# Loading the first keys by two other queues at the start of a sigmoid-attention and mixer kernel

## The chip, the cores and the metric

The kernel runs on one core of a Trainium2 chip. The metric is the device time of one execution in microseconds (us), given as the median of several runs. A core has five engines with a queue of instructions each: PE (matrix products and transposes, with its weight loads shown as PEld), DVE (vector), ACT (scalar, activation functions), POOL (general), and SP (here only issues DMAs). Sixteen DMA engines move data. SBUF is the memory on the chip that tiles live in; PSUM holds PE's results.

## The reference

Eight batches, 12 heads, 448 positions, 64 elements a head. Sigmoid attention comes first, and its result, with the heads side by side (768 columns), goes through a mixer block without normalization.

```python
def _attn_ref(q, k, v):
    S = q.shape[2]
    scale = 1.0 / np.sqrt(q.shape[-1])
    scores = scale * np.matmul(q, k.transpose(0, 1, 3, 2)) - np.log(S)
    attn = 1.0 / (1.0 + np.exp(-scores))
    return np.matmul(attn, v).astype(np.float32)

def _moe_ref(x, w_tok1, w_tok2, w_ch1, w_ch2):
    xt = x.transpose(0, 2, 1)
    h = np.maximum(xt @ w_tok1, 0.0) @ w_tok2
    u = x + h.transpose(0, 2, 1)
    h2 = np.maximum(u @ w_ch1, 0.0) @ w_ch2
    return u + h2
```

All inputs and the output are fp32. w_tok1 is 448 x 256, w_tok2 256 x 448, w_ch1 768 x 1536, w_ch2 1536 x 768.

## The kernel before, in words

The batches are worked on in five units: "A" and "B" are one batch each, and 1, 2 and 3 are two batches each. A unit is handled in pairs of heads: three pairs for A and B, six for the others. In a pair a tile holds the keys (or queries, or values) of two heads on each of two sides of the 128 partitions. A position is written as p*7+j, so that partition p holds seven rows, j = 0 to 6, and one step of the attention is one j: four matmuls of scores (L423), one sigmoid on ACT (L430) over 128 x 896 elements, and four matmuls of values (L441) that add up over j.

Keys and queries must be turned first, so that the 64 elements of a head lie across partitions. For the first seven pairs (`BY_PE = 7`) PE turns them (`turn_by_pe`, L345): 14 transposes against the identity matrix `ident`, into one PSUM bank, and one copy by DVE to SBUF. For later pairs POOL reorders the tile (`permute`, L337, tiles pk and pq) and SP issues a DMA transpose (`turn_by_dma`, L362).

Loads are issued by POOL (`load`, L238), two DMAs a tile, one for each side. The source is fp32 and the tile fp16; the DMA casts. The very first keys are loaded by `load_first` (L255) in two parts, j = 0 to 2 and j = 3 to 6 (`KEYS`), so that scores can begin on the first part. Each part is turned by `turn_first_keys` (L268): transposes, then a copy by DVE.

At the start DVE clears a tile `zero`, and PE runs nine matmuls on it (`WARM`, L1396). POOL then issues the loads of the first queries and of both parts of the first keys, makes `ident` (`make_identity`), and goes on with the values of pair 0, then keys, queries and values of pairs 1 and 2, the token weights, and unit B, the first half of the channel weight w1, and so on. From the eighth pair on, loads wait for a `gate`, a tiny copy on POOL that reads a tile made by an earlier transpose (`load_next`, L379).

The order of instructions on each engine is fixed when the program is built. A small planner writes it: it keeps a clock for each engine and one for the loads (`clock`, L125), and a table `there` of the times at which things are expected. `pool_dma(issues, cost, ...)` books a load; `did` books anything else. `first_attention` (L1320) orders unit A's attention by choosing the candidate that is expected first; `merge` (later) mixes the channel products of A and B (c_A, c_B) with the attention of the next units in the same way, and writes the stores of finished rows (`put`, tile u, to `out`) on SP. So a changed cost in the planner moves instructions without any change in what is computed. When the attention of a pair begins (`one`, j == 1), the transposes of the next pair's keys and queries are put on the list `turns`.

Of the kernel before, what the change touches and what calls it, by code (L numbers as in the profile page):

```python
# [21 lines left out]
def kernel(  # L22
# [99 lines left out]

    clock = {"pe": 1.0, "dve": 1.0, "act": 1.0, "pool": 1.0, "sp": 1.0, "load": 2.6}  # L125
    there, held = {}, set()

    def either():

        return min((2, 3), key=lambda at: there[f"m{at}"])  # L130
# [29 lines left out]
    def pe(cost, needs, gives, m="full"):  # L160
        did("pe", cost + (0.0 if m == mode[0] else 0.1), needs, gives, 0.2)
        mode[0] = m

    def dve(cost, needs, gives):
        did("dve", cost, needs, gives, 0.16)
# [4 lines left out]
    def pool_dma(issues, cost, needs, gives):  # L170
        did("pool", 0.61 * issues, needs, [])
        clock["load"] = max(clock["load"], clock["pool"] + 1.5) + cost
        for key in gives:
            there[key] = clock["load"] + 0.1
# [42 lines left out]
    def copy(engine, o, x):  # L217
        if engine == "act":
            nc.scalar.activation(out=o, in_=x, func=COPYF)  # L219
        else:  # L220
            nc.vector.tensor_copy(out=o, in_=x)
# [16 lines left out]
    def load(g, i, what):  # L238
        src = {"q": q, "k": k, "v": v}[what]
        tag, bufs = {"k": ("rk", 1), "q": ("rq", 1), "v": ("vf", 3)}[what]  # L240
        if g in SINGLE and (g, i) != ("A", 0) and what != "v":
            tag, bufs = "u", 12
        if g == "B" and what == "v":
            tag, bufs = f"s{i + 2}", 1
        t = pa.tile([128, 2, J, E], FP16, tag=tag, bufs=bufs, name=f"{what}_{g}_{i}")
        for side, (b, h) in enumerate(SIDES[g]):
            nc.gpsimd.dma_start(  # L247
                out=t[64 * side : 64 * side + 64, :, :, :],
                in_=src[b, h + 2 * i : h + 2 * i + 2].rearrange("h (p j) e -> p h j e", j=J),
            )  # L250
        raws[(g, i, what)] = t
        gated = ["gate"] if PAIRS.index((g, i)) > BY_PE else []
        pool_dma(2, 1.22, gated, [("raw", g, i, what)])

    def load_first():  # L255

        load("A", 0, "q")
        for n, (j0, j1) in enumerate(KEYS):
            t = pa.tile([128, 2, j1 - j0, E], FP16, tag=("rk", "pk")[n], bufs=1, name=f"k_A_0{n}")
            for side, (b, h) in enumerate(SIDES["A"]):  # L260
                nc.gpsimd.dma_start(
                    out=t[64 * side : 64 * side + 64, :, :, :],
                    in_=k[b, h : h + 2].rearrange("h (p j) e -> p h j e", j=J)[:, :, j0:j1, :],
                )
            pool_dma(2, 0.18 * (j1 - j0), [], [("raw", "A", 0, "k", n)])
            first_keys.append([t])

    def turn_first_keys(n):  # L268
        j0, j1 = KEYS[n]
        m = first_keys[n][0]  # L270
        t = pa.tile([128, j1 - j0, 2, P], FP16, tag="kT", bufs=2, name=f"kT_A_0{n}")
        first_keys[n].append(t)
        at = either()
        ps = bank(f"tk_A_0{n}", [128, j1 - j0, 2, P], FP16, at)
        for j in range(j1 - j0):
            for h in range(2):
                nc.tensor.transpose(
                    out=ps[64 * h : 64 * h + 64, j, :, :].rearrange("d b p -> d (b p)"),
                    in_=m[:, h, j, :],
                    identity=ident[:, :],  # L280
                )
        nc.vector.tensor_copy(out=t[:, :, :, :], in_=ps[:, :, :, :])
        pe(0.06 * (j1 - j0), [("raw", "A", 0, "k", n), f"m{at}"], ["pe"], "col")
        dve(0.56, ["pe"], [("k", "A", 0, n), f"m{at}"])

    def load_pair(g, i):
        for what in ("k", "q", "v"):
# [122 lines left out]
    def keys_of(g, i, j):  # L410
        if (g, i) == ("A", 0):
            n = int(j >= KEYS[1][0])
            return first_keys[n][1][:, j - KEYS[n][0], :, :]
        return kT[(g, i)][:, j, :, :]

    def scores(g, i, j):
# [216 lines left out]
    def begin_sum(g):  # L633
        uTs[g] = pa.tile(
            [128, NDB, S + 64], FP16, tag={"A": "ws0", "B": "ws1"}[g], bufs=1, name=f"uT_{g}"
        )
        c = S - 7 * OFF[g]
        nc.vector.memset(uTs[g][:, :, c : c + 64], 0.0)
# [463 lines left out]
    def one(g, i, j):  # L1102
        scores(g, i, j)
        at = ahead(g, i, 1)
        if j == 1 and at and PAIRS.index(at) < BY_PE:
            for what in ("k", "q"):
                turns.append(
                    ([("raw", *at, what), "m2/m3"], lambda what=what: turn_by_pe(*at, what))
                )
        after = ahead(g, i, 2)  # L1110
        if j == J - 1 and after and PAIRS.index(after) >= BY_PE:
            keys = [("raw", *after, "k"), ("raw", *after, "q")]
            loads.append((lambda: keys, lambda: turn_by_dma(*after)))
            load_next(g, i)
# [202 lines left out]
            x[3]()  # L1317
        written_later(True)

    def first_attention(sec):  # L1320


        scored = [(("A", r // J, r % J)) for r in range(3 * J)]
        valued = list(scored)
        out = [False]

        def tokens_turned():
            nc.vector.tensor_copy(
                out=w_tok2_n[:, 64:]
                .rearrange("t (c x) -> t c x", c=2)[:, :, 0:S]  # L1330
                .rearrange("t c (j p) -> t c j p", j=J),
                in_=w_tok2_s.rearrange("t c (p j) -> t c j p", j=J),
            )
            dve(0.8, ["wtok"], ["wtok2"])

        w = [(["wtok"], tokens_turned)]
        before = [0, 1]

        def begin_channels(cb):
            ch1_of("A")[0](cb)  # L1340
            begun.add(cb)

        def candidates():
            if scored:
                g, i, j = scored[0]
                keys = ["one bank", key_of(g, i, j), ("q", g, i)]
                yield keys, lambda: one(*scored.pop(0))
            soon = when(quick[0][0]) if quick else None
            if quick:
                yield quick[0][0], lambda: quick.pop(0)[1]()  # L1350
            if turns:
                yield turns[0][0], lambda: turns.pop(0)[1]()
            if w:
                yield w[0][0], lambda: w.pop(0)[1]()
            if valued and (not scored or valued[0] < scored[0]):
                g, i, j = valued[0]
                keys = [("attn", g, i, j)] + (["m0", "m1"] if j == 0 else [])
                yield keys, lambda: value_step(*valued.pop(0)[1:])
            if before and not valued:
                cb = before[0]  # L1360
                keys = [f"m{cb}", ("w1", 0), ("uT", "A", 0), ("uT", "A", 1)]
                yield keys, lambda: begin_channels(before.pop(0))
            if sec and not scored and (soon is None or ("one", "value") not in sec[0][1]):
                yield sec[0][1], lambda: sec.pop(0)[2]()

        turn_by_pe("A", 0, "q")
        turn_first_keys(0)
        turns.append(([("raw", "A", 0, "k", 1), "m2/m3"], lambda: turn_first_keys(1)))
        while scored or valued or quick and ("uT", "A", KD - 1) not in there:
            found, now = [], clock["pe"] + 0.05  # L1370
            for n, (keys, f) in enumerate(candidates()):
                t = when(keys)
                if t is not None:
                    found.append((max(t, now), n, f))
            min(found, key=lambda x: x[:2])[2]()
# [14 lines left out]
    with tc.manual_schedule(engines=None):  # L1390
        if WARM:
# [3 lines left out]
            for _ in range(WARM):  # L1395
                nc.tensor.matmul(  # L1396
                    out=ps[:, 0, :], lhsT=zero[:, 0:128], rhs=zero[:, :], start=True, stop=True
                )
        load_first()
        make_identity(nc, ident)  # L1400
        begin_sum("A")
        begin_sum("B")
        nc.vector.memset(w_tok1_t[0:64, 0, :], 0.0)
        nc.vector.memset(w_tok1_t[64:128, J, :], 0.0)
        for n in range(3):
            c = (S + 64) * n
            nc.vector.memset(w_tok2_n[:, c : c + 64], 0.0)
        load("A", 0, "v")
        load_pair("A", 1)
        load_pair("A", 2)  # L1410
# [4 lines left out]
        def load_w1(half):  # L1415
            c = slice(CH * half, CH * half + CH)
            nc.gpsimd.dma_start(
                out=w1[:, :, c], in_=moe_w_ch1.rearrange("(db d) c -> d db c", db=NDB)[:, :, c]
            )
            pool_dma(1, 6.3, [], [("w1", half)] + (["w1"] if half else []))  # L1420

        load_pair("B", 1)
        load_w1(0)
# [3 lines left out]
        nc.gpsimd.dma_start(  # L1427
            out=w2[:, :, :], in_=moe_w_ch2.rearrange("(cb c) d -> c cb d", cb=NCB)
        )
        pool_dma(1, 12.6, [], ["w2"])  # L1430
        load_pair(1, 1)

        stream = side_stream()
        ahead_of_all = [(0.0, *x) for x in stream["B"][0]]
        first_attention(ahead_of_all)
        rest = []

        main = list(rest)
# [185 lines left out]
```

## Time and profile before

| | us |
|---|---|
| median of four runs | 366.64 |
| the four runs | 366.39, 368.92, 366.28, 366.9 |
| the profiled execution, its own time | 368.22 |
| its span, from first to last instruction | 366.4 |
| mean granted clock of PE in it | 0.985 of full speed |
| HBM read / written | 43.84 MB / 11.01 MB |

A row of a timeline shows the start in us, the busy time, the engine, the line of the kernel, the operation, what it writes and reads with shapes, how many such instructions are merged (x), and in brackets how long the engine had been idle before it and what ended that. A row of waits shows an engine and line, what it waited for, the total in us, how often and the longest. The row of 40 digits on the page is the busy share of an engine in 40 equal slices of the span, in tenths.

### The profile page before, as it was taken

Reading aid. Unit: us, or ns where it says so; the run is one execution under the profiler, and the core shown is the slowest. Engines: PE = TensorE matmul, PEld = TensorE weight load, DVE = VectorE, ACT = ScalarE, POOL = GpSimd, SP = SyncE. Lnnn points to the kernel's source line nnn. Section 1 sums busy time; section 2 is a strip of 40 time slices with the busy share of each in tenths; the row PEclk is TensorE's granted clock in tenths of the full one; section 3 lists DMA queues with packets and bytes.
Section 4 is the critical chain, followed back from the end, with each engine's and each line's share of the span. In section 5 each row is a group of like instructions: output and inputs, shape, how many; then the busy total and the mean of one; then the engine's idle time right before and its main releaser. Section 6 shows DMA issues by size and latency. Waiting matters only on the chain.

```text
span 366.4 us, 7766 instructions
## 1 busy us (share of the span) xinstructions
PE 353.1 (96%) x3113; PEld 183.6 (50%) x3113; DVE 233.4 (64%) x435; ACT 197.0 (54%) x240; POOL 133.2 (36%) x213
## 2 busy tenths in 40 slices
PE   6899999999989999999999999999999999999994
PEld 2455545555444555544445556444445556455562
DVE  2177676767745578886655659775644678665863
ACT  2797356576655423288787654387887352343000
POOL 8883503565555620056565630065520000004000
PEclk9599999999999999999999999999999999999999
DMA  6999999778988955799999978899963157300153
GB/s 84 166 189 186 146 202 207 124 114 158 149 135 144 137 74 108 173 170 125 128 152 155 155 158 127 212 151 145 137 104 70 28 103 168 112 2 0 45 151 109
DMA packets 86724, 47.67 MB, mean 130 GB/s; under 512 B 61216, under 2 KB 82976, under 8 KB 86688
## 3 DMA queue, kind: packets, MB, share of 16 engines
q0 software_dynamic: 24576, 21.93, 41.8%
q1 hardware_dynamic: 61552, 23.87, 33.4%
q10 hardware_dynamic: 560, 1.38, 1.0%
q8 instruction: 24, 0.39, 0.4%
q14 instruction: 12, 0.10, 0.1%
HBM read 43.84 MB, written 11.01 MB: 150 GB/s over the span
## 4 chain that ended last, share of the span: by engine, by line
PE 70%; DMA 16%; POOL 6%; issue 2%; DVE 2%; ACT 1%; SPq 0%; POOLq 0%; ACTq 0%
PE x L742 11%; PE x L1005 9%; DMA q<-in_q_dram 6%; PE qk L423 6%; PE z L742 6%; PE xa L441 5%; PE c_B L919 4%; PE z L1005 4%; PE k L512 4%; PE yn L548 4%; DMA w<-in_moe_w_ch_dram 3%; PE c_B L861 3%; PE d L1062 3%; PE y L1005 2%; PE y L742 2%
## 5 line engine op out<-in xcount | busy, mean ns | idle before, releaser
L430 ACT ACTIVATE attn<-qk 128x896 f16<-128x896 f32 x126 | 110.5, 915 | 54.9 <-PE qk L423 47.0
L742 PEld LDWEIGHTS <-w 128*128 128x128 f16 x378 | 35.0, 98 | 39.0 <-issue 9.7
L423 PE MATMUL qk<-qT,kT 64*64 64x448 f16 x504 | 40.8, 363 | 1.8 <-DMA qT<-pq 1.3
L757 DVE COPY c<-x 128x448 f32<-128x448 f32 x42 | 26.1, 622 | 21.9 <-PE x L742 19.3
L742 PE MATMUL x<-uT,w 128*128 128x448 f16 x162 | 37.8, 353 | 0.1
L762 DVE CUSTOM_DVE_ANT_0 h2T<-z,c 128x448 f16<-128x448 f32 x36 | 22.5, 624 | 16.9 <-PE z L742 14.7
L219 ACT ACTIVATE u<-u 128x768 f16<-128x768 f32 x21 | 17.7, 843 | 25.3 <-DVE u L558 22.4
L1017 DVE TENSOR_TENSOR u<-u,x 128x384 f32<-128x384 f32 x36 | 19.9, 552 | 16.3 <-PE x L1005 16.2
L247 POOL DMA_DIRECT2D k<-in_k_dram x36 | 21.4, 602 | 22.9 <-PE tk L352 12.2
L395 POOL COPY gate<-kT 1x2 f16<-1x2 f16 x16 | 3.7, 234 | 68.0 <-DMA kT<-pk 68.0
L1005 PEld LDWEIGHTS <-h2T 128*128 128x128 f16 x216 | 20.8, 98 | 15.0 <-issue 1.6
L423 PEld LDWEIGHTS <-kT 64*64 64x64 f16 x504 | 13.6, 104 | 28.1 <-issue 26.3
L441 PE MATMUL xa<-attn,v 64*64 64x448 f16 x504 | 27.0, 349 | 0.0
L339 POOL COPY pk<-k 128x896 f16<-128x896 f16 x17 | 16.6, 974 | 26.6 <-DMA k<-in_k_dram 26.6
L430 ACT ACTIVATE attn_B<-qk_B 128x896 f16<-128x896 f32 x21 | 18.4, 915 | 14.3 <-PE qk_B L423 13.4
L742 PE MATMUL z<-s,w 128*128 128x448 f16 x108 | 24.6, 353 | 0.0
L662 POOL TENSOR_TENSOR r<-h2T,h2T 128x512 f16<-128x512 f16 x1 | 1.2, 1154 | 60.1 <-ACT h2T L231 60.1
L558 DVE TENSOR_TENSOR u<-x_nat,yn 128x384 f32<-128x384 f16 x42 | 21.1, 548 | 2.8 <-PE yn L548 2.6
L247 POOL DMA_DIRECT2D v<-in_v_dram x36 | 22.2, 642 | 1.7 <-DMA k<-in_k_dram 1.3
L430 ACT ACTIVATE attn_A<-qk_A 128x896 f16<-128x896 f32 x21 | 17.6, 923 | 9.5 <-PE qk_A L423 9.4
L339 POOL COPY pq<-q 128x896 f16<-128x896 f16 x17 | 16.1, 949 | 16.2 <-DMA q<-in_q_dram 16.0
L247 POOL DMA_DIRECT2D q<-in_q_dram x36 | 21.8, 625 | 0.1
(137 smaller groups left out, 631.0 us busy)
## 6 DMA issues: line engine op xcount, KB each, us to landing
out_dram<-u SPq DMA_DIRECT2D x49, 192.0 KB, 3.0
k<-in_k_dram POOLq DMA_DIRECT2D x36, 112.0 KB, 3.9
q<-in_q_dram POOLq DMA_DIRECT2D x36, 112.0 KB, 4.9
v<-in_v_dram POOLq DMA_DIRECT2D x36, 112.0 KB, 4.9
w<-in_moe_w_ch_dram POOLq DMA_DIRECT2D x2, 1152.0 KB, 11.5
w<-in_moe_w_ch_dram POOLq DMA_DIRECT2D x1, 2304.0 KB, 22.1
out_dram<-u ACTq DMA_DIRECT2D x7, 192.0 KB, 3.3
q_A<-in_q_dram POOLq DMA_DIRECT2D x6, 112.0 KB, 4.6
```

The lines of the kernel that those rows point to most:

```text
L219: nc.scalar.activation(out=o, in_=x, func=COPYF)
L247: nc.gpsimd.dma_start(out=t[64 * side : 64 * side + 64, :, :, :], in_=src[b, h + 2 * i : h + 2 * i + 2].rearrange("h (p j) e -> p h j e", ...
L339: nc.gpsimd.tensor_copy(out=m[:, :, :, :], in_=raws[(g, i, what)].rearrange("p h j e -> p j h e"))
L423: nc.tensor.matmul(out=ps[64 * b : 64 * b + 64, h, 0:S], lhsT=keys_of(g, i, j)[r, b, :], rhs=qT[(g, i)][r, :, b, :], start=True, stop=True,)
L430: nc.scalar.activation(out=at[:, :, :], in_=ps[:, :, 0:S], func=SIGMOID, bias=att_bias, scale=att_scale)
L441: nc.tensor.matmul(out=ps[b][64 * h : 64 * h + 64, :], lhsT=vf[r, h, j, :], rhs=attn[(g, i, j)][r, h, :], start=(j == 0), stop=(j == J - 1),)
L558: nc.vector.tensor_tensor(out=u_of(g, t)[:, DH * half : DH * half + DH], in0=x_of(g, half)[:, t, :], in1=ps[:, half, 0:DH], op=ADD,)
L742: nc.tensor.matmul(out=ps[:, :], lhsT=W(p, n, cb), rhs=A[p](n), start=(first and n == 0), skip_group_check=True, stop=(n == KD - 1),)
L757: nc.vector.tensor_copy(out=s[:, :], in_=bk[(cb, "x")][:, :])
L762: nc.vector._custom_dve(dve_ops.TENSOR_ADD_SAT, out=h[half][:, cb, S * b : S * b + S], in0=ps[:, :], in1=snap[(cb, n)][:, :], s0=BIG, s1=0.0,)
L1005: nc.tensor.matmul(out=ps[:, :], lhsT=A(p, n, kb), rhs=W(p, kb), start=(first and kb == 0), skip_group_check=True, stop=(kb == KC - 1),)
L1017: nc.vector.tensor_tensor(out=u, in0=u, in1=ps[:, :], op=ADD)
```

## The change

The first part of the first keys (j = 0 to 2) is loaded as fp32 by SP (side 0) and ACT (side 1) into a tile that uses a buffer of the tag h2T, and DVE casts it to fp16. The copy of its transposes from PSUM moves from DVE to ACT. The identity is made ahead of all of POOL's loads. POOL then loads the first queries and the second part of the keys, in this order. An activation on two columns of `zero` is put on ACT after the loads. The first part of the keys is turned before the queries; the second part is turned when the planner places it, once the first scores are written. The transposes of pair 1 are put on the list at j == 3 rather than j == 1. The planner's costs of loads are raised (a tile from 1.22 to 1.4, w1's halves from 6.3 to 6.5, w2 from 12.6 to 13.0, a part of the first keys from 0.18 to 0.2 for each j), and its load clock starts at 2.4 rather than 2.6.

```diff
-    clock = {"pe": 1.0, "dve": 1.0, "act": 1.0, "pool": 1.0, "sp": 1.0, "load": 2.6}
+    clock = {"pe": 1.0, "dve": 1.0, "act": 1.0, "pool": 1.0, "sp": 1.0, "load": 2.4}
...
-        pool_dma(2, 1.22, gated, [("raw", g, i, what)])
+        pool_dma(2, 1.4, gated, [("raw", g, i, what)])
     def load_first():
-        load("A", 0, "q")
+        got = []
         for n, (j0, j1) in enumerate(KEYS):
-            t = pa.tile([128, 2, j1 - j0, E], FP16, tag=("rk", "pk")[n], bufs=1, name=f"k_A_0{n}")
+            t = pa.tile(
+                [128, 2, j1 - j0, E],
+                FP16 if n else FP32,
+                tag="pk" if n else "h2T",
+                bufs=1 if n else 2,
+                name=f"k_A_0{n}",
+            )
             for side, (b, h) in enumerate(SIDES["A"]):
-                nc.gpsimd.dma_start(
+                engine = nc.gpsimd if n else nc.scalar if side else nc.sync
+                engine.dma_start(
                     out=t[64 * side : 64 * side + 64, :, :, :],
                     in_=k[b, h : h + 2].rearrange("h (p j) e -> p h j e", j=J)[:, :, j0:j1, :],
                 )
-            pool_dma(2, 0.18 * (j1 - j0), [], [("raw", "A", 0, "k", n)])
-            first_keys.append([t])
+            got.append(t)
+            if n:
+                pool_dma(2, 0.2 * (j1 - j0), [], [("made", n)])
+            else:
+                did("sp", 0.56, [], [("raw", "A", 0, "k")], 2.9)
+                clock["load"] += 0.2 * (j1 - j0)
+                load("A", 0, "q")
+        return got
+
+    def cast_keys(f):
+        t = pa.tile(list(f.shape), FP16, tag="rk", bufs=1, name="k_A_0")
+        nc.vector.tensor_copy(out=t[:, :, :, :], in_=f[:, :, :, :])
+        dve(0.35, [("raw", "A", 0, "k")], [("made", 0)])
+        return t
...
-        nc.vector.tensor_copy(out=t[:, :, :, :], in_=ps[:, :, :, :])
-        pe(0.06 * (j1 - j0), [("raw", "A", 0, "k", n), f"m{at}"], ["pe"], "col")
-        dve(0.56, ["pe"], [("k", "A", 0, n), f"m{at}"])
+        pe(0.06 * (j1 - j0), [("made", n), f"m{at}"], ["pe"], "col")
+        engine = ("act", "dve")[n]
+        copy(engine, t[:, :, :, :], ps[:, :, :, :])
+        evac(engine, 64 * (j1 - j0), ["pe"], [("k", "A", 0, n), f"m{at}"])
+        first_keys.append(t)
...
-        if j == 1 and at and PAIRS.index(at) < BY_PE:
+        if j == (3 if (g, i) == ("A", 0) else 1) and at and PAIRS.index(at) < BY_PE:
...
-            if turns:
+            if turns and len(scored) < 3 * J:
                 yield turns[0][0], lambda: turns.pop(0)[1]()
...
-        turn_by_pe("A", 0, "q")
-        turn_first_keys(0)
-        turns.append(([("raw", "A", 0, "k", 1), "m2/m3"], lambda: turn_first_keys(1)))
+        turns.append(([("made", 1), "m2/m3"], lambda: turn_keys(1, first[1])))
...
-        load_first()
         make_identity(nc, ident)
+        first = load_first()
+        made = pa.tile([128, 2], FP16, tag="gate", bufs=2, name="first_act")
+        nc.scalar.activation(out=made[:, :], in_=zero[:, 0:2], func=SIGMOID)
...
+        turn_keys(0, cast_keys(first[0]))
+        turn_by_pe("A", 0, "q")
         load("A", 0, "v")
...
-            pool_dma(1, 6.3, [], [("w1", half)] + (["w1"] if half else []))
+            pool_dma(1, 6.5, [], [("w1", half)] + (["w1"] if half else []))
...
-        pool_dma(1, 12.6, [], ["w2"])
+        pool_dma(1, 13.0, [], ["w2"])
```

More of the change, by code (lines that the diff above doesn't have):

```diff
@@ L264, in load_first, with turn_keys @@
                 )
-            pool_dma(2, 0.18 * (j1 - j0), [], [("raw", "A", 0, "k", n)])
-            first_keys.append([t])
-    def turn_first_keys(n):
+            got.append(t)
[11 more added lines that the diff above has]
+        return t
+    def turn_keys(n, m):
         j0, j1 = KEYS[n]
-        m = first_keys[n][0]
+        at = either()
         t = pa.tile([128, j1 - j0, 2, P], FP16, tag="kT", bufs=2, name=f"kT_A_0{n}")
-        first_keys[n].append(t)
-        at = either()
         ps = bank(f"tk_A_0{n}", [128, j1 - j0, 2, P], FP16, at)
@@ L412, in keys_of @@
             n = int(j >= KEYS[1][0])
-            return first_keys[n][1][:, j - KEYS[n][0], :, :]
+            return first_keys[n][:, j - KEYS[n][0], :, :]
         return kT[(g, i)][:, j, :, :]
@@ L1318, in merge, with first_attention @@
         written_later(True)
-    def first_attention(sec):
+    def first_attention(sec, first):
         scored = [(("A", r // J, r % J)) for r in range(3 * J)]
@@ L1434 @@
         ahead_of_all = [(0.0, *x) for x in stream["B"][0]]
-        first_attention(ahead_of_all)
+        first_attention(ahead_of_all, first)
         rest = []
```

## The prediction

> **What bounds the kernel now.** I read the page first. The span is 366.4 us and PE is busy for 353.1 us of it, so the end is set by how soon PE gets dense work and how rarely it is stopped.
>
> ```profile
> PE 353.1 (96%) x3113; PEld 183.6 (50%) x3113; DVE 233.4 (64%) x435; ACT 197.0 (54%) x240; POOL 133.2 (36%) x213
> ...
> PE   6899999999989999999999999999999999999994
> ```
>
> Each digit is 9.2 us. Only the first two and the last of PE's row show room, apart from one 8. Hence the second view, PE's waits: first from 0 to 10 us, then 10 to 20, then 95 to 120.
>
> ```profile
> PE warm L1396 <- DVE zero L1393: 1.2, 1, 1.2
> PE tq_A L352 <- POOL ident masks.py:199: 0.9, 1, 0.9
> PE tk_A L277 <- DMA k_A<-in_k_dram: 0.7, 1, 0.7
> PE qk_A L423 <- ACT attn_A L430: 0.7, 1, 0.7
> ...
> PE tk_A L352 <- DMA k_A<-in_k_dram: 0.7, 1, 0.7
> ...
> PE qk L423 <- DMA qT<-pq: 1.3, 2, 1.0
> ```
>
> Columns: total us, times, longest. The opening stops are each under 1 us; from 20 to 95 us PE waits for about 0.8 us in all; then one transfer, a DMA transpose, stops it for 1.3 us; after 120 us four stops make 1.3 us. With a further 0.9 us on ACT in the second stretch that is 8.5 us in all, 1.2 of them before the first matmul, so some 7 us at most can be won without less work or a faster clock. Third, the timeline of the opening:
>
> ```profile
> 1.25 1.35 POOL L247 DMA_DIRECT2D q_A<-in_q_dram  x2 [0.80 <-POOLq L1608]
> 2.58 2.39 POOL L261 DMA_DIRECT2D k_A<-in_k_dram  x4
> 4.90 0.28 POOL masks.py:197 MEMSET ident<- 128x128 f16 x1
> 5.60 0.58 PE L352 MATMUL tq_A<-ident,q_A 128*64 128x128 f16 x14 [0.93 <-POOL ident masks.py:199]
> 7.34 0.61 PE L277 MATMUL tk_A<-ident,k_A 128*64 128x128 f16 x8 [0.70 <-DMA k_A<-in_k_dram]
> 8.52 3.34 ACT L430 ACTIVATE attn_A<-qk_A 128x896 f16<-128x896 f32 x4 [6.50 <-PE qk_A L423]
> 11.93 0.96 PE L352 MATMUL tk_A<-ident,k_A 128*64 128x128 f16 x14 [0.67 <-DMA k_A<-in_k_dram]
> ```
>
> The queries' tile was there at 4.97 (PE's weight load of q_A ended a wait on that DMA), but the identity, queued on POOL behind six DMA issues, was not until 5.54. Then k's second part held PE, in order, until 7.34, and the scores at 7.88 stand behind it. Fourth, the chain of waits that ended last, around 108 us:
>
> ```profile
> 103.20 0.95 POOL pq L339
> 104.15 0.88 SPq L367
> 105.13 2.90 DMA qT<-pq
> 108.03 0.14 issue
> 108.16 0.38 PE qk L423 x4
> ```
>
> It runs through loads and transposes from 54.4 us to here, and then along PE. Last, stretches of 1 us: the granted clock is 0.50 in each from 8 to 17 us, 0.70 in 7 to 8 and 0.68 in 17 to 18. PE thus ran at half speed from about 7.4 to 17.6 us.
>
> [...]
>
> **The change, part by part.**
>
> *The dummy activation.* The table is loaded at 0.74 us already, 6.5 us ahead of its use. The load moves behind one DMA issue on ACT (0.59 us, half of the 1.17 us that SP takes for two), so to 1.3 to 2.6 us; the activation adds about 0.2. Worth 0: ACT has nothing before about 5.2 us. If that cover were gone, up to 0.8 us would show.
>
> *First keys.* POOL loses two issues, 1.16 us. SP and ACT issue one each from about 0.7 us, ending at 1.3; both queues were empty. No hardware load is in the trace. Bounds from issue to landing: 2.7 us (the shortest of k_A's) to 4.6 us (the median of q_A's six). I take 3.0, the median of SP's 192 KB stores: landed at 3.7. The cast on DVE: 0.35 us, as the 128x384 copy of L282 takes, between 0.2 and 0.5; DVE is free from 2.4 us, and nothing waits behind it but the later copies. Cast done at 4.1. PE reaches the six transposes at 4.7 as warming ends (0.36 us). They stand ahead of the queries', so a landing after about 5.2 would delay those. The copy goes to ACT: from ACT's 128x896 and 128x448 copies (0.92 and 0.55 us) 0.83 ns a column, so 0.49 us for 384; done near 5.6.
>
> *Identity first.* 0.6 us of POOL go ahead of the queries. POOL then issues q at 1.9 (was 1.25), k's second part at 3.2 (3.74), v at 4.4 (5.49). q lands at 4.97+0.6=5.6; 14 transposes 0.6, copy 0.62: scores at about 6.9, against 7.88, and attn_A starts near 7.5 against 8.52. That is 1.0 us earlier.
>
> *What is late next.* The order of PE's instructions now has the transposes of pair 1's keys ahead of one group of values, and they wait for k_A's next load. It landed at 11.9 and was issued 1.1 us later than it now will be, but DMA was nearly full from 3 us on (share 0.9 to 1.1 in stretches of 1 us, one of 0.69). The data in front of it is the same 0.9 MB, less 0.2 MB written by another queue (98 KB of fp16 before). Hidden wholly: 0 us gained; issued-limited: 1.1. I take 0.6: lands at 11.3. The value group now behind it costs 0.35 us at half clock. So pair 1 is ahead by 0.3 to 0.8, mid 0.5, where the opening had promised 1.0. From 15.2 us ACT is dense until 24.5 and PE fills around it, so 0.5 us is kept in the main, although PE's own part of it, won at half clock, is worth half.
>
> *The planner's numbers.* Loads are priced dearer (1.22 to 1.4, w1 6.3 to 6.5, w2 12.6 to 13.0). No instruction of PE is added or lost; the order differs in about the first 2/5 of it. Ahead of the scores of pairs 2 to 5 of unit 1 there are now 10 to 12 more matmuls of 128x384 or 128x448 than before (counted in the two orders), at 0.16 to 0.19 us about 2 us. The wait at 108 us was 1.0 and another 0.3. Both should go: 0 to 1.3, I take 0.9. On SP the stores of u_1 and u_2 move ahead of kT of pairs 4 and 5, 1.2 us of issue each; their chains on PE also end sooner by two score groups, and kT was waiting for pk at 91.7 and 102.9, so I price them at 0. If u_1 came late, kT would be late by the same, minus the 2 us.
>
> *The sum.* 0.5 + 0.9 = 1.4 us. The profiled span would be 365.0 from 366.4; that execution took 368.22, 1.8 around its span, and is 1.6 above the median of the four runs, 366.64. I apply the difference to the median: **365.2 us**; own range 364.3 (0.8 + 1.3 + 0.2 of further PE stops) to 366.2.
>
> **Rivals.**
> 1. [...]
> 2. *Transfers hide it.* k_A's next load lands when it did, and the stall at 108 us follows the loads: 366.6 (366.2 to 367.2). For it: a full DMA. Against: the added work in front of the scores.
> 3. *The clock returns later,* the slow side. PE waits longer for k in its new place, 10 to 11.3 us[...]. [...] One of the four runs, 368.92, shows that 2 us more occurs.
>
> **How the numbers follow.** Likeliest 0.52, rival 1 0.18, rival 2 0.16, rival 3 0.14. A measurement of this kernel tells about 0.5%, 1.83 us, from no change, so faster means under 364.8: rival 1 and a third of the likeliest case, 0.36. Slower, over 368.5: rival 3 with a little of others, 0.15. The rest 0.49. The range 363.8 to 367.6 leaves out rival 3 and a part of rival 1.
>
> **What would show it.** Right: first attn_A near 7.5 us; pair 1's first transposes at 11.0 to 11.6; no wait of scores on qT near 108; POOL's v issues near 4.4. Wrong: k's cast after 5.2 us, PE cold past 18 us, or a score waiting for a transpose that SP issues behind a store of u.

## The result, and the profile after

| | before | after |
|---|---|---|
| median beside each other, us | 367.75 (55 runs) | 367.56 (36 runs) |
| ratio after / before, 95% interval | | 0.9999, 0.9983 to 1.0014 |
| profiled execution, own time / span, us | 368.22 / 366.4 | 366.33 / 364.5 |
| granted clock of PE in it | 0.985 | 0.998 |

The forecast was 365.2 us, 1.4 us below the median of four runs (366.64). The measurement shows no difference. Medians in this document are of all runs; the ratios leave out the few that were more than 1.5% above the fastest run of their kernel. The unchanged kernel after was measured twice more beside before, with ratios of 0.9978 [0.9961, 0.9996] and 0.9976 [0.9958, 0.9994]. The three, weighted by their intervals (worked out here), give 0.9986 [0.9976, 0.9995]: about half a microsecond less, a third of the forecast. The four runs had also been a low draw of before: its median of 55 runs is 1.1 us higher.

The page of the kernel after: busy time of each engine, and the rows of 40 slices of PE and of its clock. PE is 2 us less busy than before (351.1 against 353.1) with the same count of instructions, and the clock row has no cold slice.

```profile
PE 351.1 (96%) x3113; PEld 182.4 (50%) x3113; DVE 233.2 (64%) x435; ACT 197.6 (54%) x242; POOL 130.8 (36%) x211
...
PE   6799999999999999999999999999999999999994
...
PEclk9999999999999999999999999999999999999999
```

Timeline of the opening of after (start, busy time, engine, line, operation; the bracket is the idle time before it and what ended that):

```profile
0.73 0.20 POOL masks.py:197 MEMSET ident<- 128x128 f16 x1 [0.29 <-POOLq L1629]
0.74 0.74 SPq L268 DMA_DIRECT2D k_A<-in_k_dram  x1
1.51 1.28 ACT L1419 ACT_TABLE_LOAD   x1 [1.51 <-PEq L1629]
3.64 0.51 DVE L283 CAST k_A<-k_A 128x384 f16<-128x384 f32 x1 [1.52 <-DMA k_A<-in_k_dram]
5.61 0.58 PE L371 MATMUL tq_A<-ident,q_A 128*64 128x128 f16 x14 [0.33 <-DMA q_A<-in_q_dram]
6.91 0.57 PE L442 MATMUL qk_A<-qT_A,kT_A 64*64 64x448 f16 x8 [0.71 <-DVE qT_A L376]
7.34 3.35 ACT L449 ACTIVATE attn_A<-qk_A 128x896 f16<-128x896 f32 x4 [1.52 <-PE qk_A L442]
10.11 0.58 PE L371 MATMUL tk_A<-ident,k_A 128*64 128x128 f16 x14 [0.60 <-DMA k_A<-in_k_dram]
```

The opening went almost as forecast: the keys are cast well before PE ends its warming, the queries are turned at once, and the first sigmoid starts at 7.34 us where it had been 8.52. PE's waits of after, from 0 to 10 us and then from 10 to 20 (total us, times, longest):

```profile
PE warm L1413 <- DVE zero L1410: 1.2, 1, 1.2
PE qk_A L442 <- ACT attn_A L449: 0.7, 2, 0.5
PE qk_A L442 <- DVE qT_A L376: 0.7, 1, 0.7
PE tq_A L371 <- DMA q_A<-in_q_dram: 0.3, 1, 0.3
```

```profile
PE tk_A L371 <- DMA k_A<-in_k_dram: 1.2, 2, 0.6
PE qk_A L442 <- ACT attn_A L449: 1.0, 4, 0.4
```

The stops on ident and on the second part of the first keys are gone. In their place the keys of the next pairs (`tk_A`) wait twice for their loads, 1.2 us in all, where before had one such wait of 0.7. From 95 to 120 us this execution has no wait of PE at all; the stop of scores on qT is gone here. What the waits don't say, the chain that ended last does. Its longest pieces in after (start, us, what), up to 15 us:

```profile
1.44 1.35 POOL q_A L247 x2
2.79 1.19 POOL k_A L268 x2
3.97 1.19 POOL v_A L247 x2
5.16 1.18 POOL k_A L247 x2
6.34 1.19 POOL q_A L247 x2
7.53 1.19 POOL v_A L247 x2
9.17 5.74 DMA k_A<-in_k_dram
15.04 0.58 PE tk_A L371 x14
```

The first scores are not in it. The chain goes along POOL's queue of DMA issues, through one load of 5.74 us to the transposes at 15.04 us, and from there mostly along PE and ACT. Before, it began alike, but it stays with issues and loads up to 37 us, where the first half of w1 lands and PE's first channel products c_A start (same view of before, a part):

```profile
5.55 1.15 POOL v_A L247 x2
6.70 1.19 POOL k_A L247 x2
7.89 1.19 POOL q_A L247 x2
9.07 0.50 POOL v_A L247
9.57 5.20 DMA v_A<-in_v_dram
...
15.63 6.66 DMA w_tok_s<-in_moe_w_tok_dram
...
25.49 11.60 DMA w<-in_moe_w_ch_dram
...
37.13 0.93 PE c_A L861 x4
```

So these lines could have been read in advance: PE's first scores, where the change was to make its gain, were not on the path. POOL's issues, which are on it, do come earlier with the change (those of the first values at 3.97 us, before 5.55).

### The profile page after: what moved, and what is told of

It is laid out like the page before. It is cut to its first block, busy times and chain, and to the rows that moved or that the text cites. A ratio compares the mean times of both kernels' runs of the same rounds, so it can differ in the third digit from the quotient of the medians.

```text
span 364.5 us, 7773 instructions
## 1 busy us (share of the span) xinstructions
PE 351.1 (96%) x3113; PEld 182.4 (50%) x3113; DVE 233.2 (64%) x435; ACT 197.6 (54%) x242; POOL 130.8 (36%) x211
## 4 chain that ended last, share of the span: by engine, by line
PE 84%; DMA 6%; DVE 3%; ACT 3%; POOL 2%; issue 1%; ACTq 0%; POOLq 0%; DVEq 0%
PE x L761 12%; PE qk L442 9%; PE x L1024 7%; PE xa L460 7%; PE z L761 6%; PE c_B L938 4%; PE c_B L880 4%; PE c_A L880 4%; PE k L531 4%; PE z L1024 4%; PE c_A L938 3%; PE d L1081 3%; DMA uT<-u 3%; PE yn L567 3%; PE y L761 2%; PE y L1024 2%
## 5 line engine op out<-in xcount | busy, mean ns | idle before, releaser
L761 PEld LDWEIGHTS <-w 128*128 128x128 f16 x378 | 35.0, 98 | 39.3 <-issue 10.0
L761 PE MATMUL x<-uT,w 128*128 128x448 f16 x162 | 37.8, 353 | 0.1
L761 PE MATMUL z<-s,w 128*128 128x448 f16 x108 | 24.6, 353 | 0.0
L681 POOL TENSOR_TENSOR r<-h2T,h2T 128x512 f16<-128x512 f16 x1 | 1.2, 1152 | 60.6 <-ACT h2T L231 60.6
L1024 PEld LDWEIGHTS <-r 128*128 128x128 f16 x162 | 15.5, 98 | 11.0 <-issue 1.2
## 6 DMA issues: line engine op xcount, KB each, us to landing
w<-in_moe_w_ch_dram POOLq DMA_DIRECT2D x2, 1152.0 KB, 10.6
```

The source lines that it names most:

```text
L761: nc.tensor.matmul(out=ps[:, :], lhsT=W(p, n, cb), rhs=A[p](n), start=(first and n == 0), skip_group_check=True, stop=(n == KD - 1),)
L1024: nc.tensor.matmul(out=ps[:, :], lhsT=A(p, n, kb), rhs=W(p, kb), start=(first and kb == 0), skip_group_check=True, stop=(kb == KC - 1),)
```

## The experiments

Each was timed beside runs of the kernel before; 14 to 22 runs of each kernel unless said. Ratios are to before.

### Both kernels again, and the two halves of the change

**before_again** and **after_again** have no edit. **opening_only** is after with the old costs, **costs_only** is before with the new ones:

```diff
-        pool_dma(2, 1.4, gated, [("raw", g, i, what)])
+        pool_dma(2, 1.22, gated, [("raw", g, i, what)])
...
-            pool_dma(1, 6.5, [], [("w1", half)] + (["w1"] if half else []))
+            pool_dma(1, 6.3, [], [("w1", half)] + (["w1"] if half else []))
...
-        pool_dma(1, 13.0, [], ["w2"])
+        pool_dma(1, 12.6, [], ["w2"])
```

This is opening_only's edit of after; costs_only is the reverse of it, made on before. The planner's entries for the first keys themselves (0.2 for each j, the load clock's start at 2.4) belong to the opening here and go with it.

> The kernel before, once more, for a second trace and more times. Theory 1 (clock): the profiled execution of before owed most of its 1.9 us over after to its 10.2 us at half clock; an execution without that stretch has a span of 364.5 to 365.2 us, and one with it about 366.4. Theory 2 (given back): before is slower than after by 1.4 us up to some place and catches up after it, whatever the clock; then its span at a mean clock of 0.995 or more is still 366 us or more and after's extra time is seen in a wait that before doesn't have. Ratio to before 1.000 +- 0.002 on both.

> The changed kernel, once more. Theory 1: when its clock has a cold stretch its span is 366 us or more, although the first sigmoid still starts near 7.3 us. Theory 2: its lead at 30 us is 1.5 us or more in every trace and is gone at the end where the clock was the same. Ratio to before 0.998 to 1.002.

> The changed kernel with the planner's costs of loads as they were (1.22, 6.3, 12.6): the opening alone. Theory 1: the opening is worth little at the end: 0.996 to 1.001. Theory 2: if the dearer costs give the gain back, this one is faster than before by 0.8 us or more, 0.998 or less; the wait of scores on qT near 108 us comes back, 1 to 2 us.

> The kernel before with the planner's costs of loads raised as in the change (1.4, 6.5, 13.0), its opening untouched. Theory 1: the wait near 108 us is gone, worth up to 1.3 us by the trace of before: 0.9965 to 1.000. Theory 2: slower than before by 0.5 to 1.5 us, 1.001 to 1.004, since the dearer costs write other work in front of loads that were there in time.

| | median us | ratio |
|---|---|---|
| before_again | 367.96 | 0.9996 [0.9963, 1.0029] |
| after_again | 367.31 | 0.9978 [0.9961, 0.9996] |
| opening_only | 368.53 | 1.0018 [0.9997, 1.0038] |
| costs_only | 368.51 | 1.0007 [0.9981, 1.0032] |

Within these intervals the new opening alone gains nothing, and the new costs alone gain nothing. Only together are they a little faster than before. The intervals of after_again and opening_only just fail to meet; those of after_again and costs_only overlap, so that half of the statement is weaker. In the trace of costs_only PE waits neither for qT nor for w1, and its time is still that of before. And the stop on qT, absent in the profiled execution of after, is back in that of after_again, though its instructions are the same (PE's waits, 95 to 120 us):

```profile
PE qk L442 <- DMA qT<-pq: 0.9, 1, 0.9
```

The stop belongs to an execution, not to the order of instructions alone.

### Is the opening on the path? (before_warm, after_delay, after_delay24)

**before_warm** puts filler matmuls into PE's gaps in the opening of the kernel before. **after_delay** puts 8 fillers of 512 columns ahead of the first scores of after, **after_delay24** puts 24 there.

First before_warm (two fillers ahead of the second part's transposes, two ahead of the scores of j == 2), then after_delay:

```diff
-    WARM = 9
+    WARM = 11
...
+        if n:
+            filler(2, 0)
...
+        if (g, i) == ("A", 0) and j == 2:
+            filler(2, 0)
```

```diff
+        if (g, i, j) == ("A", 0, 0):
+            for _ in range(8):
+                nc.tensor.matmul(
+                    out=extra[0][:, :], lhsT=zeros[0][:, 0:128], rhs=zeros[0][:, :], start=True, stop=True
+                )
```

> The kernel before with matmuls on the cleared tile put into PE's gaps of the opening: two more in the warming (11), two ahead of the transposes of the keys' second part, two ahead of the scores of j = 2; nothing is ordered otherwise, and the opening's loads are untouched. Clock theory: what the change gains at the end is only a clock that goes cold less often. Then this one has a mean clock of 0.995 or more, against 0.991 for before, and gains as much as the change did: 0.996 to 0.999. Opening theory: the earlier scores are worth 1 us by themselves; then this one is at 0.999 or more, and stays 0.8 us behind the changed kernel at equal clock (365.2 us of span).

> The changed kernel with eight matmuls on the cleared tile ahead of the first scores: PE is busy with them from 6.2 to about 7.9 us, so the first scores come at 7.9, not 6.9, as late as before, with the clock kept busy. Clock theory: the same time as the changed kernel to 0.3 us, a span of 365.0 to 365.5 where the mean clock is 0.9965 or more; ratio 0.996 to 0.999. Opening theory: 0.7 to 1.0 us slower than the changed kernel, ratio 0.999 to 1.002.

> after_delay with 24 filler matmuls instead of 8: the first scores start about 4 us later than in the kernel after (near 11 us). Theory 'the opening has a slack of 1 to 1.5 us, up to the arrival of the keys of pair 1, and behind it PE's time counts in full': 2.5 to 3.2 us above the kernel after (367.1 to 367.6 us), ratio to before 1.005 to 1.008. Theory 'the load stream up to 66 us sets the end whatever PE does early': below 1.001.

| | first scores in the trace, us | median us | ratio |
|---|---|---|---|
| before_warm | 8.0 | 367.8 | 1.0019 [1.0000, 1.0039] |
| after_delay | 8.4 | 366.39 | 0.9975 [0.9956, 0.9994] |
| after_delay24 (6 runs) | 11.6 | 370.16 | 1.0068 [1.0042, 1.0093] |

In before_warm the granted clock was 1.00 from 0 to 20 us, where before's profiled execution had 0.50 from 8 to 17; over its timed runs it was 0.9955 in the mean against 0.9909 for before beside it (means worked out here), and nothing was won. Its trace shows where the lead goes: the first scores of unit B start at 28.6 us (30.0 and 29.4 in the two executions of before), but the first c_A at 37.0 (37.1 and 37.2), after a wait of 1.3 us for w1.

In after_delay the first scores start later than in any profiled execution of before or of its variants with the same opening (7.6 to 7.9, before_warm 8.0), and the time is that of after: 0.4 us less, give or take 0.8, worked out from its ratio and the 0.9986 of after with their intervals. After_delay24 does pay: the same difference, times 367.8, is 3.0 us, give or take 1.0, for a start that is 4.1 to 4.7 us later than in after's executions (6.9 to 7.5). What takes up the small delay is the wait for the next keys: PE turned these at 10.1, 11.3 and 10.3 us in the three executions of after, each time after a wait for their load, at 10.95 without one in after_delay, and only in after_delay24 clearly later (timelines of the two):

```profile
10.95 0.58 PE L371 MATMUL tk_A<-ident,k_A 128*64 128x128 f16 x14
```

```profile
14.09 0.58 PE L371 MATMUL tk_A<-ident,k_A 128*64 128x128 f16 x14
```

So in this order the first scores have a slack of about 1 us, which after_delay shows. An estimate from after_delay24 is 1 to 2 us, if PE counts in full past the slack; two sizes of delay can't show both. No such delay was tried in the order of before. The chain of after_delay24 shows the path turned:

```profile
5.77 0.58 PE tq_A L371 x14
6.35 5.29 PE warm L1126 x24
11.63 0.34 PE qk_A L442 x4
```

Now the fillers and the first scores are the chain, and POOL's issues are not in it. The theory that the load stream up to 66 us sets the end whatever PE does falls with this.

### Is the chain of loads and transposes on the path? (splits and early loads)

**before_split** and **after_split** load w2 in halves, the second behind the loads of pair (1,1). **before_early**, **after_early** and **after_early_delay** load the keys and queries of pair (1,1) ahead of w2, in two unused buffers of tag u. The planner is told the old times, so PE's order is unchanged; after_early_delay has the 8 fillers besides.

First the edit of the two splits, then that of the early loads:

```diff
-            out=w2[:, :, :], in_=moe_w_ch2.rearrange("(cb c) d -> c cb d", cb=NCB)
+            out=w2[:, 0:KC, :], in_=moe_w_ch2.rearrange("(cb c) d -> c cb d", cb=NCB)[:, 0:KC, :]
...
         load_pair(1, 1)
+        nc.gpsimd.dma_start(
+            out=w2[:, KC:NCB, :], in_=moe_w_ch2.rearrange("(cb c) d -> c cb d", cb=NCB)[:, KC:NCB, :]
+        )
```

```diff
-        if g in SINGLE and (g, i) != ("A", 0) and what != "v":
+        if (g in SINGLE and (g, i) != ("A", 0) or (g, i) == (1, 1)) and what != "v":
             tag, bufs = "u", 12
...
         load_w1(1)
...
+        load(1, 1, "k")
+        load(1, 1, "q")
...
-        load_pair(1, 1)
+        load(1, 1, "v")
```

> The kernel before with the load of w2 in two halves, the second after the loads of pair 1 of unit 1; the order on PE, DVE, ACT and SP is the same. Theory 3 (loads): between 54 and 108 us PE meets a chain of loads and transposes that starts behind w2's 2.3 MB and takes no notice of the opening, so a lead there is lost to waits. Then the first DMA transpose of keys is issued at 58 to 61 us, not 65.5, the wait of scores on qT near 108 us is under 0.3 us, and the ratio is 0.996 to 0.999. Else the first transpose moves and the time doesn't, 0.999 to 1.001.

> The changed kernel with w2's load in two halves as in before_split. Theory 3: with the chain out of the way the opening's lead reaches the end: 0.993 to 0.997, at least 0.7 us under before_split and 0.8 under the changed kernel. Clock theory: no lead was lost to the chain: at equal clock the same span as before_split to 0.3 us, and the ratio 0.996 to 0.999.

> The kernel before, with the loads of keys and queries of pair (1,1) put ahead of the load of the second channel weights w2 on POOL's queue, in two buffers of their own (tag u) instead of the shared rk and rq; the planner is given the old times, so the order on PE, VectorE, ScalarE and SyncE is the old one. Theory 'chain of loads' (the end is set by load, permute and DMA transposes of the pairs after 54 us): the first transposing DMA of pair (1,1)'s keys starts well before 65 us, PE's waits on qT between 60 and 120 us (0 to 2 us in the earlier traces) go, and the median falls by about 1 us, ratio 0.995 to 0.999. Theory 'PE alone' (the end is PE's sum from the first scores on): ratio 1.000, within 0.002. If w2's own arrival was what counted, it is now 1 us later and the ratio is 1.002 to 1.004.

> The same edit of loads on the kernel after. Theory 'chain of loads': with the chain out of the way the opening's lead of about 0.5 to 1 us reaches the end, so this kernel is below before_early by that and below the kernel after: ratio to before 0.994 to 0.997. Theory 'PE alone': as the kernel after, ratio 0.998 to 1.000, and not different from before_early by more than these two differ without the edit (0 to 0.2%).

> after_early with eight filler matmuls ahead of the first scores, which start about 1 us later, as in after_delay. Theory 'chain of loads': with the chain relieved the first microseconds count, so it is 0.5 to 1 us above after_early. Theory 'the lead is taken up by waits anyway' (w1 near 37 us, or others): the same as after_early within 0.15%.

| | median us | ratio |
|---|---|---|
| before_split (6 runs) | 371.05 | 1.0089 [1.0058, 1.0120] |
| after_split (8 runs) | 370.26 | 1.0083 [1.0055, 1.0112] |
| before_early | 368.19 | 1.0003 [0.9982, 1.0025] |
| after_early | 366.71 | 0.9974 [0.9957, 0.9992] |
| after_early_delay | 366.65 | 0.9967 [0.9952, 0.9982] |

The split was meant to relieve the chain and did the opposite. A transposing DMA that SP issued at 61.2 us, 4.6 us after POOL issued the second half of w2, took 4.06 us of issue, where the same one takes 1.23 in before; in after_split it took 4.35 (views of tile qT, issues of SP from 50 to 75 us, first before_split, then before):

```profile
L367 SPq DMA_TRANSPOSE qT<-pq x1: 4062/4062/4062, 61.2 to 61.2; - x1
```

```profile
L367 SPq DMA_TRANSPOSE qT<-pq x1: 1228/1228/1228, 67.0 to 67.0; - x1
```

The early loads did relieve it. In before_early PE's waits from 20 to 95 us are only these, and from 95 to 120 us there are none:

```profile
PE qk_A L423 <- ACT attn_A L430: 0.5, 2, 0.3
PE xb_A L474 <- DVE uT_A L654: 0.3, 1, 0.3
```

Still the timed runs gained nothing that can be measured, though w2 landed no later in the trace (62.7 us in before_early, 63.2 in before). So taking away the wait on qT, 1.3 us in one trace, was worth nothing measurable, while before_split, where the chain is pushed back (the gate of unit B at 70.5 us against 68.2 in before) and PE waits 3.5 us for qT, is 0.9% slower, some 3 us. Of all kernels after_early_delay has the lowest ratio; its interval overlaps those of after, so it isn't shown to beat that.

### Does PE run into w1? (w1late, w1soon, both)

In three traces the first channel products c_A waited for the first half of w1: 0.8 us in before_again, 1.3 in before_warm and in opening_only. In these three, as in before, the chain that ended last runs along loads up to c_A. Example, the two largest of PE's waits of before_warm from 20 to 120 us:

```profile
PE qk L433 <- DMA qT<-pq: 1.7, 2, 0.9
PE c_A L871 <- DMA w<-in_moe_w_ch_dram: 1.3, 1, 1.3
```

In after, the planner has put c_A behind 28 value products xa_B, and there is no such wait. Of its three executions, two have a chain that leaves the loads by 15 us; that of after_again still goes through w1, to xa_B at 37.0 us. The next kernels move c_A by shifting one entry of the planner, the time at which it expects the first half of w1: **before_w1late** (+1 us) and **opening_w1late** (opening_only, +4) to behind xa_B, **after_w1soon** (-2) to ahead of it. **after_third** is after, unchanged. **before_both** and **opening_both** join w1late with the early loads.

```diff
             pool_dma(1, 6.3, [], [("w1", half)] + (["w1"] if half else []))
+            if not half:
+                there[("w1", 0)] += 1.0
```

> The kernel before with one number of the planner changed: the first half of w1 is entered 1 us later, which puts the first channel products c_A behind the block of 28 value products xa_B instead of ahead of it; loads and everything up to about 35 us are the same. Theory 'w1' (PE runs into the arrival of w1's first half near 37 us, so that whatever it gained before is waited away there): no wait of c_A for the DMA of w, c_A starts after 38.5 us, keys of pair (1,0) (tile tk) are turned before 53 us where the earlier traces of before had 53.4 to 53.6, and the ratio is 0.997 to 0.9985. Theory 'noise and the later chain': 1.000 within 0.0015.

> opening_only (the new opening with the old planner costs; it had 368.53 us and a wait of 1.3 us of c_A for w) with the first half of w1 entered 4 us later, which puts c_A behind xa_B as in the kernel after. Theory 'w1': no wait of c_A for w, and the time falls to that of the kernel after or below, 366.6 to 367.4 us, ratio 0.996 to 0.999. Theory 'the other costs matter' (those of the loads of keys, queries and values): it stays near opening_only, ratio 1.001 to 1.003.

> The kernel after with the first half of w1 entered 2 us earlier, which puts the first 18 channel products c_A ahead of xa_B, as in the kernel before. Theory 'w1': c_A starts near 36 us after a wait of 1 us or more for the DMA of w, and the time is 0.7 to 1.5 us above the kernel after of the same call, ratio to before 1.000 to 1.004. Theory 'noise and the later chain': as the kernel after, within 0.3 us.

> The kernel after, unchanged, on the chip of these runs, so that the three others can be set against it: ratio to before 0.996 to 1.000, no wait of c_A for w.

> before_w1late (first channel products c_A behind xa_B, no wait for w1) together with before_early (keys and queries of pair (1,1) loaded ahead of w2), each of which alone left the time where it was (1.0011 and 1.0003). Theory 'two waits in series' (PE waits for w1 near 37 us or, if it comes through there earlier, for the transposed queries qT between 60 and 115 us; either takes what the other gives): with both out of the way the time falls, ratio 0.996 to 0.9985, no wait for w or qT over 0.5 us in the trace. Theory 'neither is on the path': 1.000 to 1.002.

> opening_w1late (which had a wait of 2.6 us for qT and a ratio of 1.0046) with keys and queries of pair (1,1) loaded ahead of w2. Theory 'two waits in series': the wait for qT goes and the ratio falls to 0.996 to 0.999. Theory 'neither is on the path', or the order of the old planner costs is worse for another reason: 1.003 to 1.006.

| | median us | ratio |
|---|---|---|
| before_w1late | 368.13 | 1.0011 [0.9987, 1.0035] |
| opening_w1late | 369.1 | 1.0046 [1.0025, 1.0067] |
| after_w1soon | 368.86 | 1.0043 [1.0021, 1.0064] |
| after_third | 367.06 | 0.9976 [0.9958, 0.9994] |
| before_both | 367.34 | 1.0001 [0.9980, 1.0022] |
| opening_both | 368.18 | 1.0024 [1.0004, 1.0043] |

Putting c_A back ahead of xa_B in after costs 1.8 us (368.86 against 367.06, intervals apart), and its timeline has the wait:

```profile
34.91 1.69 PE L880 MATMUL c_A<-uT_A,w 128*128 128x448 f16 x8 [1.16 <-DMA w<-in_moe_w_ch_dram]
```

So in after's order this move costs, with the wait that it brings. But the converse fails: with c_A behind xa_B and no wait for w1, before and opening_only are no faster (the order of opening_w1late brought a wait of 2.6 us on qT with it). "Two waits in series" falls too, since before_both has neither wait in its trace and the time of before. Opening_both's median is 0.9 us below opening_w1late's, with overlapping intervals. So the order that the new costs make is worth 1 to 2 us to the new opening (after_again against opening_only, after_third against after_w1soon). Moving c_A back loses it, but moving c_A alone doesn't make it.

## Why the prediction was right or wrong

**The opening: right, slightly large.** Scores at "about 6.9" came at 6.91. The cast took 0.51 us (forecast 0.35) and started at 3.64 (3.7): harmless, as PE warmed until 5.0. The dummy activation cost nothing: the table load ran from 1.51 to 2.79 us, 1.28 us as in before, and ACT then stood idle for 2.31 us until the copy of the keys at 5.33. The copy of 384 columns on ACT took 0.49 us as worked out. But 1.0 us was one execution against one: first scores came at 6.9, 7.5 and 7.5 in the three profiled executions of after, and at 7.9 and 7.8 in the two of before, so the lead is nearer 0.5. That one execution came at 6.91 exactly was luck.

**"What is late next": the right row, the wrong reading.** The next keys were indeed late, and in two executions of three they came earlier than I took (PE turned them at 10.1, 11.3 and 10.3, forecast 11.0 to 11.6; before, 11.9 and 11.6). POOL's issue for them moved from 6.70 to 5.16 us, while the loads in the two chains shown took 5.20 us before and 5.74 after.

**The step that failed first: "so 0.5 us is kept in the main".** I carried the lead on because PE is 96% busy. It is not kept: the opening alone (opening_only) is 0.7 us slower than before by its ratio, from 0.1 us faster to 1.4 slower by its interval. The delays show the first part of the reason, in the order of after: the first scores can start 1 us later at no cost, because PE then waits for the next keys. But the lead that remains at these keys (opening_only turns them at 10.6 us) isn't kept either. Here the chains tell a part: with the old order they follow the loads up to 37 us in before, and PE's lead runs into a wait for w1, 1.3 us in opening_only. I had read the chain around 108 us only. Where the rest of the lead goes is open; see the end. The remark that time "won at half clock is worth half" was too generous as well: in before the half clock cost nothing that can be measured (before_warm, ratio 1.0019).

**The second: "Both should go: 0 to 1.3, I take 0.9".** In the one trace they went, and I would have called this right; after_again had 0.9 us of it back, and before_early and costs_only, with none, were no faster. The term measured as 0: before_early's interval, times 367.8, allows from 0.7 us less to 0.9 us more. One profiled execution's wait was treated as a property of the kernel.

**"I apply the difference to the median".** To forecast by a difference was sound, but 366.64 stood 1.1 us under the median of the longer series. The 55 runs scatter by 1.25 us (standard deviation), more than the effect.

**The planner's numbers.** They were priced only for the scores behind the added matmuls. What the experiments show is elsewhere: with the new opening the new costs are worth 1.2 us (367.31 against 368.53), with the old opening nothing. That this is near the 0.9 I took is luck, as the wait that I priced isn't what makes it. I had no term for it, and it is what is left of the gain.

**The rivals.** Rival 1, 364.2, was a clock that returns earlier than in before; when it would return and what that would be worth was the author's estimate, which no trace shows. There is no cold stretch in the trace of after (granted clock 1.00 from 0 to 20 us), more than rival 1 asked for, but that was worth nothing measurable in before (before_warm), and 364.2 is not reached. It isn't a property of the kernel either: after_third's profiled execution has a mean clock of 0.995 against 0.998 in after, and one of its 22 timed runs has 0.986, where before's with its cold stretch has 0.985. "Transfers hide it" (366.6) gave about the measured difference, but by another mechanism: the next keys landed earlier than before. The third, a clock that returns later than before's 17.6 us, is not in the traces of after and after_again (1.00 from 10 to 20 us in both); the mean of 0.995 in after_third, over 365.5 us, leaves room for at most about 4 us at half clock (worked out here). What a later return would cost was an estimate that no run shows.

**Open.** First, the end of the kernel, which I didn't price. From the first x at L742, at 151.8 us in before (L761 in after), PE has the same instructions in the same order in all 20 traces. From there to the end the eight traces with before's opening take 214.7 to 214.9 us, the twelve with the new opening 215.1 to 215.4. So about 0.5 us is lost there with the new opening, as much as the whole measured gain; why, no run shows. Second, why kernels with no wait over 0.5 us after 20 us in their trace (before_early, before_both) have the times of before. The profiled execution of before_early had a span of 364.9 us where the median of its timed runs was 366.4, so what holds a typical one back is in no trace. Third, which of the moves in the order of the new costs makes the 1.2 us.

## What to carry to other kernels

Before pricing a gain at the start of a kernel, follow the chain that ended last from its very first microsecond; if the instruction that you speed up is not in it, its gain may be slack, however busy its engine is over the whole span. A cheap proof is to delay it by filler work, in two sizes: what costs nothing was slack, and a size that costs bounds the amount. A wait of a microsecond that one profiled execution shows is to be looked for in a second one before it is priced.

## What the runs showed of the hardware

A transposing DMA that SP issued 4.6 us after a load of 1152 KB took 4.06 us of SP's time instead of 1.23, and landed 10.1 us after its issue instead of 2.9 (before_split against before, where the two loads of that size took 11.4 and 11.6 us to land); in after_split, 5.1 us after the load, it took 4.35. The issue of the same first half of w1 on POOL began between 23.6 and 25.5 us in profiled executions of after that have the same instructions (after_third 23.6, after 23.9, after_again 25.5). And the half clock at the start of before (0.50 from 8 to 17 us in its profiled execution), in a stretch where the chain runs along loads and issues, cost no time that these measurements can tell (before_warm, 1.00 from 0 to 20 us, ratio 1.0019, 1.0000 to 1.0039).
